# Attention two blocks at a time over two groups, with results in place

## The chip, the cores and the metric

One core of a Trainium2 chip runs the whole program. The metric is the device time of one execution in microseconds (us). The engines are PE (matrix products), DVE (vector), ACT (activations), POOL and SP, which issues the transfers. Each works through its own instructions in program order and waits on the others by semaphores.

## The reference

```python
# attention within chunks of 64: q, k, v are (8, 8, 576, 64)
scores = scale * np.matmul(q_c, k_c.transpose(0, 1, 2, 4, 3))
scores = scores - np.max(scores, axis=-1, keepdims=True)
attn = np.exp(scores)
attn = attn / (np.sum(attn, axis=-1, keepdims=True) + 1e-09)
out = np.matmul(attn, v_c)
# x: (4608, 512) from out
h = x @ w_in                     # 512 -> 2048
x2 = (h * np.cos(h)) @ w_out     # 2048 -> 512
a = x2 @ w1; b = x2 @ w2         # 512 -> 1024 each
y = ((a * b) @ w3) @ w_out2      # all float32
```

## The kernel before

The 4608 tokens are nine tiles of 512 (`TT`); a tile is four blocks of 128 tokens, and a block is two chunks of 64 for eight heads. Float32 products run as three products of split numbers (`mm3`, L104: high x high, high x low, low x high), so that an operand always has a high part (ACT copies it) and a low part (DVE or POOL subtracts).

The program has three parts. The first pass goes over all nine tiles with five of the eight weight groups each (`GA`, 45 groups in all); the second goes over the tiles with the other three; the last applies the second network. One group makes two halves of h (`d` and `e`), takes cos (`chain_t`, `chain_r`, `chain_cos`, `chain_g`: ACT, DVE, ACT, DVE), splits g = h cos h (`split_g`, copies on ACT, subtractions on POOL at L570), and one group later multiplies g with `w_out` in two output products `x` and `y` of 12 matmuls of 512 columns. h is formed with full products in the first two tiles (steps P, Q) and from tile 2 on with seven smaller ones (steps 1, 2, 5, 3 of 6, 12, 12, 12 matmuls of 256 columns).

The order of all instructions is written out: each group runs a string (`ORDER0` in tile 0, `ORDER1P` in tile 1, `ORDER1` in tiles 2 to 7; an E stands for the last group of a tile), one letter per step. Lower-case `a c b d` and capitals `A C B D` are the cos chain, `s` splits the previous group's g, `v` converts weights (tile 0), `l m h r` prepare later weights in four steps on ACT and DVE, `M H R` make sums of weights, `S T o` prepare the next tile's x.

Attention runs ahead of the products. Blocks 0 to 3 are done at the start (`START`). In each of the first four groups of a tile, one block of the next tile goes through five steps, at the five letters `q`:

- A, `att_scores` (L355): 32 matmuls 64x64x64 into two PSUM banks; for each of two banks a maximum over 64 (DVE, L367) and a subtraction (L369) into `ex`
- B, `att_softmax` (L373): the exponential, 512 elements per partition, in place (ACT, L375)
- E, `att_scale` (L377): sum, add, reciprocal (DVE), and the division, a multiplication on POOL (L384)
- C, `att_transpose` (L387): four transposes on PE (L391) and a copy on ACT into a second tile `pt` (L393)
- D, `att_values` (L396): 32 matmuls 64x64x64 (L404) and two copies of 256 elements into `xf` (ACT, L409)

In tiles 2 to 7, A stands between steps 2 and 5, B and E behind step 5, C between the two output products, D behind the second. The exponential and the sine use different tables on ACT, and a load of the table stands ahead of each change. q and k of a block are loaded on SP's queue at A of a block before, v at D of the block before.

PSUM has eight banks: four of `acc`, two of `h`, and two (`at`) that attention uses in turn for scores, transposes and values.

Of the kernel before, what the change touches and what calls it, by code (L numbers as in the profile page):

```python
# [9 lines left out]
F32 = mybir.dt.float32  # L10
# [4 lines left out]
ALU = mybir.AluOpType  # L15
# [41 lines left out]
def chunk_attention_two_ffn(  # L57
# [276 lines left out]
    qk_at = [0]  # L334

    def load_qk(j):
        qk_at[0] = j + 1
        qks[j] = t = wk.tile([P, 2, 2 * HP, 64], F32, tag="qk", name="qk")
        nc.sync.dma_start(out=t[:, 0], in_=q[j])
        nc.sync.dma_start(out=t[:, 1], in_=k[j])  # L340

    def load_v(j):
        vs[j] = vt = one.tile([P, 2, HP, 64], F32, tag="v", name="vt")
        for c in range(2):
            nc.sync.dma_start(out=vt[64 * c:64 * c + 64], in_=v[j].rearrange("(e t) c h d -> c t e h d", e=2)[c])

    def banks_of(j, early, name):
        return [(ps_acc.tile([P, HP, P], F32, tag=f"acc{2 * (j % 2) + c}", name=f"{name}{c}") if early and name == "ps_s"  # L350
                 else ps_h.tile([P, HP, P], F32, tag="h", name=f"{name}{c}") if early
                 else ps_at.tile([P, HP, P], F32, tag="at", name=f"{name}{c}"))[:, 0:2].rearrange("p a (b k) -> p (a b) k", k=64)
                for c in range(2)]

    def att_scores(j, early):  # L355
        qk = qks.pop(j)
        ps = banks_of(j, early, "ps_s")
        for h in range(2 * HP):
            for c in range(2):
                r, o = slice(64 * c, 64 * c + 64), 64 * (c ^ (h % 2))  # L360
                nc.tensor.matmul(ps[c][o:o + 64, h // 2], qk[r, 0, h], qk[r, 1, h], start=True, stop=True)
        while qk_at[0] < min(NJ, j + 2 + early):
            load_qk(qk_at[0])
        mx = small.tile([P, HP, 2], F32, tag="mx", name="mx")
        ex = wk.tile([P, HP, 2, 64], F32, tag="ex", name="ex")
        for c in range(2):
            nc.vector.reduce_max(out=mx[:, :, c], in_=ps[c], axis=AX.X)  # L367
        for c in range(2):
            nc.vector.tensor_tensor(out=ex[:, :, c], in0=ps[c], op=ALU.subtract,  # L369
                                    in1=mx[:, :, c].unsqueeze(2).to_broadcast([P, HP, 64]))  # L370
        att[j] = ex.rearrange("p h c k -> p (h c) k")

    def att_softmax(j, early):  # L373
        ex = att[j]
        nc.scalar.activation(ex, ex, AF.Exp, scale=SCALE)  # L375

    def att_scale(j, early):  # L377
        ex = att[j]
        sm = small.tile([P, 2 * HP], F32, tag="sm", name="sm")
        nc.vector.reduce_sum(out=sm, in_=ex, axis=AX.X)  # L380
        nc.vector.tensor_scalar_add(sm, sm, 1e-9)
        rc = small.tile([P, 2 * HP], F32, tag="rc", name="rc")
        nc.vector.reciprocal(rc, sm)
        (nc.vector if early else nc.gpsimd).tensor_tensor(  # L384
            out=ex, in0=ex, in1=rc.unsqueeze(2).to_broadcast([P, 2 * HP, 64]), op=ALU.mult)

    def att_transpose(j, early):  # L387
        ex = att[j]
        ps = bank(early)
        for h in range(HP):  # L390
            nc.tensor.transpose(ps[:, P * h:P * h + P], ex[:, 2 * h:2 * h + 2].rearrange("p e k -> p (e k)"), ident)  # L391
        pt = wk.tile([P, HP, P], F32, tag="ex", name="pt")
        nc.scalar.activation(pt, ps.rearrange("p (h t) -> p h t", h=HP), AF.Copy)  # L393
        att[j] = pt

    def att_values(j, early):  # L396
        pt = att.pop(j)
        ps = banks_of(j, early, "ps_v")
        vt = vs.pop(j)
        for h in range(HP):  # L400
            for e in range(2):
                for c in range(2):
                    r, o = slice(64 * c, 64 * c + 64), 64 * (c ^ e)
                    nc.tensor.matmul(ps[c][64 * e:64 * e + 64, h], vt[r, e, h], pt[r, h, o:o + 64], start=True, stop=True)  # L404
        n, jj = divmod(j, TT // P)
        if j + 1 < NJ:
            load_v(j + 1)
        for c in range(2):
            nc.scalar.activation(xf[:, :, P * jj + 64 * c:P * jj + 64 * c + 64], ps[c], AF.Copy)  # L409
        if jj == TT // P - 1 and n < NTILE - 1 and n not in xs:  # L410
            nc.sync.dma_start(out=xd[n], in_=xf)

    def att_tok(step, early):
        (att_scores, att_softmax, att_scale, att_transpose, att_values)["ABECD".index(step[0])](int(step[1:]), early)

    OPS = ("B11", "B21", "T2", "T1", "T3", "B22", "T4")
# [177 lines left out]
    def half_tile(c, name):  # L602
        return (one.tile([P, TT], F32, tag=("v", "x4")[c - 2], name=name) if c >= 2
                else wk.tile([P, TT], F32, tag="ex", name=name))

    xa = {}

    def load_x2a(n, c):
        xa[n, c] = t = half_tile(c, "x2a")
        nc.sync.dma_start(out=t, in_=x2a[n][c])  # L610


# [34 lines left out]

    def load_wf(f):
        if f in (2, 3):
            parts = tuple(wk.tile([P, TT], F32R, tag=("t", "ex")[f - 2], name="wf") for _ in range(2))  # L650
# [104 lines left out]
    with tc.manual_schedule():  # L755
# [10 lines left out]
        for tok in START.split():  # L766
            if tok == "x":
                conv_tick()
            elif tok == "o":
                x_op(plain.pop(0))  # L770
            else:
                att_tok(tok, True)

        def order_of(i, nth, end):
            if i < GA:
                return ORDER0E if end else ORDER0
            if i < 2 * GA:
                return ORDER1PE if end else ORDER1P
            if i <= iA:
                return ORDER1E if end else ORDER1  # L780
# [4 lines left out]
        steps = [s + str(j) for j in range(4, NJ) for s in "ABECD"]  # L785
        NG = len(groups)
        iA, iB = (NTILE - 1) * GA, NTILE * GA
        n_sums = 0
# [1 line left out]
        for i in range(NG):  # L790
# [35 lines left out]
            for op in order_of(i, nth, end):  # L826
# [26 lines left out]
                elif op in "1253PQ":  # L853
                    getattr(z, "step" + op)()
                elif op in "ac":
                    chain_t(i, z.d if op == "a" else z.e, "ac".index(op))
                elif op in "AC":
                    chain_r(i, z.d if op == "A" else z.e, "AC".index(op))
                elif op in "bd":
                    chain_cos(i, "bd".index(op))  # L860
                elif op in "BD":
                    chain_g(i, z.d if op == "B" else z.e, "BD".index(op))
                elif op == "q":
                    if i < iA and nth < 4:
                        att_tok(steps[20 * n + 5 * nth + n_q], False)
                    elif i >= iB + FOLD and fq < 4 * FB2:
                        need(("w3", fq // 2), *(("wo2", j) for j in range(FB2)))
                        fold(fq // 4, fq % 4)
                        fq += 1
                        if fq == 4 * FB2:  # L870
                            load_wf(0)
                            load_wf(1)
                    n_q += 1
                elif op in "ST":
                    x_sums("ST".index(op))
                elif op == "o":
                    if i < GA and not n_o:
                        x_plain()
                    x_op((z.done if i < GA or i >= 2 * GA else OPS)[n_o], n + 1 if ps == 0 else None)
                    n_o += 1  # L880
# [138 lines left out]
```

## Time and profile before

| | us |
|---|---|
| median of 3 runs | 1495.42 (1493.06 to 1502.28) |
| profiled execution | 1492.33 |
| its span in the trace | 1490.5 |

| engine | busy us | share of the span |
|---|---|---|
| PE | 1444.5 | 97% |
| DVE | 1094.4 | 73% |
| ACT | 687.4 | 46% |
| POOL | 264.7 | 18% |

The span is the time from the first to the last instruction of the profiled execution. Attention ends at about 545 us of it. PE's granted clock over the span is 0.989 of full; it is lower only in the first slices of the page (7, 8 and then 9 tenths or more). A busy PE counts from the start of a matmul to its modelled end; matmuls overlap, so the distance from one start to the next tells what one costs.

### The profile page before, as it was taken

The numbers are of one execution on the slowest core, as the hardware profiler recorded it, in microseconds if no ns is written. First come the engines' busy times: TensorE is split into PE (matmuls) and PEld (weight loads), VectorE is DVE, ScalarE is ACT, GpSimd is POOL, SyncE is SP. The second block draws the span as 40 slices with busy tenths as digits, with TensorE's granted clock in tenths as the row PEclk, the third lists the DMA queues.
The fourth block names the chain that finished last, engine by engine and source line by source line (L and its number), as shares of the span: only waits on it lengthen the run. The fifth ranks groups of instructions, "written<-read, shape, count | busy, mean of one in ns | idle before, by whom it ended". The sixth has DMA issues, their size and how long they took to land.

```text
span 1490.5 us, 26018 instructions
## 1 busy us (share of the span) xinstructions
PE 1444.5 (97%) x9996; PEld 1247.3 (84%) x9996; DVE 1094.4 (73%) x1844; ACT 687.4 (46%) x1173; POOL 264.7 (18%) x194
## 2 busy tenths in 40 slices
PE   5889999999999999999999999999999999999998
PEld 4778878888888889988888889998888888888887
DVE  6986789898898887777777777676565666656553
ACT  4776677777777775444444444231032023014002
POOL 0222222222222222211222222122000100200000
PEclk7899999999999999999999999999999999999999
DMA  7664656565664718999989684586435542641501
GB/s 247 205 206 142 214 175 216 168 242 186 220 229 145 248 65 290 372 336 322 312 290 343 243 305 144 196 328 247 148 113 192 169 148 109 224 148 59 212 34 57
DMA packets 122812, 307.38 MB, mean 206 GB/s; under 512 B 13632, under 2 KB 25664, under 8 KB 121536
## 3 DMA queue, kind: packets, MB, share of 16 engines
q1 hardware_dynamic: 122688, 305.71, 58.9%
q8 instruction: 79, 1.29, 0.3%
q14 instruction: 45, 0.37, 0.1%
HBM read 210.50 MB, written 95.16 MB: 205 GB/s over the span
## 4 chain that ended last, share of the span: by engine, by line
PE 77%; DVE 12%; ACT 4%; DMA 3%; issue 2%; POOL 1%; SPq 0%; DVEq 0%; ACTq 0%; POOLq 0%
PE acc L106 10%; PE acc L107 10%; PE acc L108 10%; PE ps_hh L106 10%; PE ps_hh L108 10%; PE ps_hh L107 9%; PE ps_aa L106 5%; PE ps_aa L107 5%; PE ps_aa L108 5%; ACT L375 2%; PE ps_v L404 1%; DVE ex L369 1%; DVE t L552 1%; POOL ex L384 1%; DVE sm L380 1%
## 5 line engine op out<-in xcount | busy, mean ns | idle before, releaser
L570 POOL TENSOR_TENSOR g<-t,g 128x512 fp32r<-128x512 f32 x144 | 198.9, 1402 | 557.8 <-ACT g L569 519.0
L106 PE MATMUL acc<-g,w 128*128 128x512 f32 x576 | 228.5, 397 | 0.0
L107 PE MATMUL acc<-g,w 128*128 128x512 f32 x576 | 225.9, 392 | 0.0
L108 PE MATMUL acc<-g,w 128*128 128x512 f32 x576 | 225.0, 391 | 0.0
L108 PE MATMUL ps_hh<-T,w 128*128 128x256 f32 (+1 forms) x616 | 181.8, 295 | 4.6 <-DVE w L199 4.6
L106 PE MATMUL ps_hh<-T,w 128*128 128x256 f32 (+1 forms) x616 | 184.7, 300 | 0.0
L107 PE MATMUL ps_hh<-T,w 128*128 128x256 f32 (+1 forms) x616 | 181.4, 295 | 0.0
L108 PEld LDWEIGHTS acc<-g,w 128*128 128x128 f32 x576 | 108.5, 188 | 23.6
L107 PEld LDWEIGHTS acc<-g,w 128*128 128x128 f32 x576 | 109.0, 189 | 19.9 <-POOL g L570 0.6
L106 PEld LDWEIGHTS acc<-g,w 128*128 128x128 f32 x576 | 108.9, 189 | 19.7
L108 PEld LDWEIGHTS ps_hh<-T,w 128*128 128x128 f32 x616 | 118.2, 192 | 7.7 <-DVE w L199 5.2
L106 PE MATMUL ps_hh<-B,w 128*128 128x256 f32 (+1 forms) x396 | 120.2, 304 | 3.7 <-DVE t L561 2.9
L106 PEld LDWEIGHTS ps_hh<-T,w 128*128 128x128 f32 x616 | 118.2, 192 | 5.4
L107 PEld LDWEIGHTS ps_hh<-T,w 128*128 128x128 f32 x616 | 118.3, 192 | 3.2
L107 PE MATMUL ps_hh<-B,w 128*128 128x256 f32 (+1 forms) x396 | 116.5, 294 | 0.0
L108 PE MATMUL ps_hh<-B,w 128*128 128x256 f32 (+1 forms) x396 | 116.3, 294 | 0.0
L744 ACT ACTIVATE phl<-e 128x512 fp32r<-128x512 f32 x32 | 20.2, 632 | 201.2 <-DVE e L742 201.2
L557 ACT ACTIVATE t<-t,half_pi 128x512 f32<-128x512 f32 x144 | 98.3, 715 | 1.4
L106 PE MATMUL acc<-wf,phl 128*128 128x512 f32 x252 | 98.2, 390 | 0.0
L107 PE MATMUL acc<-wf,phl 128*128 128x512 f32 x252 | 98.1, 389 | 0.0
L108 PE MATMUL acc<-wf,phl 128*128 128x512 f32 x252 | 98.0, 389 | 0.0
L547 ACT ACTIVATE t<-d 128x512 int32<-128x512 f32 x62 | 38.9, 627 | 120.6 <-DVE d L501 120.6
(199 smaller groups left out, 3417.4 us busy)
## 6 DMA issues: line engine op xcount, KB each, us to landing
w<-sd SPq DMA_DIRECT2D x159, 512.0 KB, 5.9
sd<-raw SPq DMA_DIRECT2D x104, 256.0 KB, 4.7
s<-sd SPq DMA_DIRECT2D x43, 256.0 KB, 5.2
qk<-in_q_dram SPq DMA_DIRECT2D x36, 256.0 KB, 4.4
qk<-in_k_dram SPq DMA_DIRECT2D x36, 256.0 KB, 4.6
vt<-in_v_dram SPq DMA_DIRECT2D x72, 128.0 KB, 3.2
x2a<-x2o SPq DMA_DIRECT2D x36, 256.0 KB, 3.2
x2a<-x2a SPq DMA_DIRECT2D x36, 256.0 KB, 5.6
```

The costliest lines, as they stand in the source:

```text
L106: nc.tensor.matmul(ps, a[0], b[0], start=first, stop=False)
L107: nc.tensor.matmul(ps, a[0], b[1], start=False, stop=False)
L108: nc.tensor.matmul(ps, a[1], b[0], start=False, stop=last)
L369: nc.vector.tensor_tensor(out=ex[:, :, c], in0=ps[c], op=ALU.subtract, in1=mx[:, :, c].unsqueeze(2).to_broadcast([P, HP, 64]))
L375: nc.scalar.activation(ex, ex, AF.Exp, scale=SCALE)
L380: nc.vector.reduce_sum(out=sm, in_=ex, axis=AX.X)
L384: (nc.vector if early else nc.gpsimd).tensor_tensor(out=ex, in0=ex, in1=rc.unsqueeze(2).to_broadcast([P, 2 * HP, 64]), op=ALU.mult)
L404: nc.tensor.matmul(ps[c][64 * e:64 * e + 64, h], vt[r, e, h], pt[r, h, o:o + 64], start=True, stop=True)
L547: nc.scalar.activation(t.bitcast(I32), h, AF.Copy, scale=INV2PI, bias=0.25)
L557: nc.scalar.activation(t, t, AF.Sin, scale=TWO_PI, bias=half_pi)
L570: nc.gpsimd.tensor_tensor(out=lo, in0=r, in1=f32(hi), op=ALU.subtract)
L744: nc.scalar.activation(t[:, 0], e0, AF.Copy)
```

## The change

Blocks 4 to 35 go in pairs: the first two groups of a tile take one pair, the next two another. The even group has one step (letter 6: scores of both blocks), in tiles 1 to 7 between its two output products and in tile 0 at its end. The odd group has the other four (7, 8, 9, 0): exponential right behind the split of g, division behind step 5 (or Q), transposes between the output products, values at the end. In the even group's string of tiles 1 to 7, the product of the first half with its cosine (`B`) now stands ahead of the weight step `m`, and `d` behind it.

One operation on DVE, ACT and POOL covers both blocks: two maxima and two subtractions of 512 elements per pair, one exponential, one sum and one division of 1024, two copies of 512 into `xf`. Transposes are copied per block, back into `ex`, which has one buffer of 4 KB in place of two of 2 KB. Both v of a pair are loaded right after the scores into a buffer of q and k; q and k of the next pair are loaded one after the scores and one after the values. The four early blocks keep their step order, and write to two unused weight slots. Tiles of later passes that shared the two `ex` buffers are halves of the one now; the small tiles have one buffer.

```diff
-ORDER0 = "PsvaAqQvqcCqxybBdvDqvq"
+ORDER0 = ("PsvaAQvcCxybBdvD6v", "Ps7vaAQ8vcCx9ybBdvD0v")
-ORDER1P = "PsqMhQqqHaclAxqbCrRmBdyqDL"
+ORDER1P = ("PsMhQHaclAxbCrRBm6dyDL", "Ps7MhQ8HaclAx9bCrRmBdy0DL")
-ORDER1 = "1s2qMh5qqHa3clAxqbCrRmBdyqDL"
+ORDER1 = ("1s2Mh5Ha3clAxbCrRBm6dyDL", "1s72h58Ha3clAx9bCrRmBdy0DL")
...
-    small = ctx.enter_context(tc.tile_pool(name="small", bufs=2))
+    small = ctx.enter_context(tc.tile_pool(name="small", bufs=1))
...
+    def load_v2(j):
+        vt = wk.tile([P, 2, 2, HP, 64], F32, tag="qk", name="vt2")
+        for b in range(2):
+            vs[j + b] = vt[:, b]
+            fill_v(vt[:, b], j + b)
...
+    def less_max(ex, ps):
+        g = ex.shape[1]
+        mx = small.tile([P, 2, g], F32, tag="mx", name="mx")
         for c in range(2):
+            nc.vector.reduce_max(out=mx[:, c], in_=ps[c], axis=AX.X)
...
+    def over_sum(ex, eng):
+        e = ex.rearrange("p g c k -> p (g c) k")
...
+        eng.tensor_tensor(out=e, in0=e, in1=rc.unsqueeze(2).to_broadcast([P, g, 64]), op=ALU.mult)
...
+    def turn(ex, ps):
         for h in range(HP):
+            nc.tensor.transpose(ps[:, P * h:P * h + P], ex[:, h].rearrange("p e k -> p (e k)"), ident)
+        nc.scalar.activation(ex.rearrange("p h c k -> p (h c k)"), ps, AF.Copy)
...
+    def pair_tok(step, j):
+        if step == "A":
+            att[j] = ex = wk.tile([P, 2 * HP, 2, 64], F32, tag="ex", name="ex", bufs=1)
+            ps = pair_banks("ps_s")
+            for b in range(2):
+                scores_mm(qks.pop(j + b), ps, b)
+            load_v2(j)
+            if j + 2 < NJ:
+                load_qk(j + 2)
+            less_max(ex, ps)
+        elif step == "B":
+            nc.scalar.activation(att[j], att[j], AF.Exp, scale=SCALE)
+        elif step == "E":
+            over_sum(att[j], nc.gpsimd)
+        elif step == "C":
+            for b in range(2):
+                turn(att[j][:, HP * b:HP * b + HP], bank(False))
+        else:
+            ex = att.pop(j)
+            ps = pair_banks("ps_v")
+            for b in range(2):
+                values_mm(ex[:, HP * b:HP * b + HP], vs.pop(j + b), ps, b)
+            if j + 3 < NJ:
+                load_qk(j + 3)
...
+            for c in range(2):
+                nc.scalar.activation(x[:, c], ps[c].rearrange("p (b h) k -> p b h k", b=2), AF.Copy)
...
+        if c == 0:
+            t = wk.tile([P, 2, TT], F32, tag="ex", name="x2a", bufs=1)
...
+                elif op in "67890":
+                    if i < iA and nth < 4:
+                        pair_tok("ABECD"["67890".index(op)], 4 * n + 4 + nth // 2 * 2)
```

## Rows read from the trace of the kernel before

**Rows 1.** Part 1 of the page: busy us (share of span) and instructions of each engine.

```profile
PE 1444.5 (97%) x9996; PEld 1247.3 (84%) x9996; DVE 1094.4 (73%) x1844; ACT 687.4 (46%) x1173; POOL 264.7 (18%) x194
```

**Rows 2.** Stretches: length, busy PE, PEld, DVE, ACT, POOL; clock, DMA share, GB/s.

```profile
34.20:111.08 76.88, 65.35 (x620) 58.22 (x619) 72.13 (x119) 54.64 (x91) 18.23 (x14) 0.93 0.66 214
111.08:168.20 57.12, 54.16 (x562) 46.63 (x561) 39.82 (x84) 39.05 (x66) 14.57 (x13) 1.00 0.47 150
420.10:481.87 61.77, 61.54 (x605) 53.31 (x604) 52.82 (x97) 46.34 (x77) 18.10 (x15) 1.00 0.57 197
```

**Rows 3.** Part 4 of the page: shares of the chain that ended last, by line.

```profile
PE acc L106 10%; PE acc L107 10%; PE acc L108 10%; PE ps_hh L106 10%; PE ps_hh L108 10%; PE ps_hh L107 9%; PE ps_aa L106 5%; PE ps_aa L107 5%; PE ps_aa L108 5%; ACT L375 2%; PE ps_v L404 1%; DVE ex L369 1%; DVE t L552 1%; POOL ex L384 1%; DVE sm L380 1%
```

**Rows 4.** PE's timeline around one block: start us, us, engine, line, operation, out<-in, count.

```profile
455.93 0.28 PE L108 MATMUL ps_hh<-T,w 128*128 128x256 f32 x1
456.14 0.69 PE L361 MATMUL ps_s<-qk 64*64 64x64 f32 x32
456.76 0.39 PE L106 MATMUL ps_hh<-T,w 128*128 128x256 f32 x1
456.98 0.28 PE L107 MATMUL ps_hh<-T,w 128*128 128x256 f32 x1
457.10 0.28 PE L108 MATMUL ps_hh<-T,w 128*128 128x256 f32 x1
...
462.26 0.39 PE L108 MATMUL acc<-g,w 128*128 128x512 f32 x1
462.73 0.66 PE L391 MATMUL ps_at<-ident,ex 128*128 128x128 f32 x4
463.14 0.47 PE L106 MATMUL acc<-g,w 128*128 128x512 f32 x1
463.45 0.39 PE L107 MATMUL acc<-g,w 128*128 128x512 f32 x1
...
465.76 0.39 PE L108 MATMUL acc<-g,w 128*128 128x512 f32 x1
466.08 0.69 PE L404 MATMUL ps_v<-pt,vt 64*64 64x64 f32 x32
466.70 0.39 PE L106 MATMUL ps_hh<-B,w 128*128 128x256 f32 x1
466.93 0.28 PE L107 MATMUL ps_hh<-B,w 128*128 128x256 f32 x1
```

**Rows 5.** The other engines' timeline in the same block.

```profile
455.85 2.53 POOL L570 TENSOR_TENSOR g<-t,g 128x512 fp32r<-128x512 f32 x2 [6.06 <-ACT g L569]
...
456.90 0.75 DVE L367 TENSOR_REDUCE mx<-ps_s 128x4 f32<-128x256 f32 x2
...
458.39 1.28 ACT L375 ACT_TABLE_LOAD   x1 [1.64 <-DVE ex L369]
...
458.50 0.69 DVE L499 TENSOR_TENSOR e<-d,ps_hh 128x512 f32<-128x512 f32 x1 [0.18 <-PE ps_hh L108]
...
459.22 0.42 DVE L501 TENSOR_TENSOR d<-e,ps_hh 128x256 f32<-128x256 f32 x1
...
460.35 0.69 DVE L380 TENSOR_REDUCE sm<-ex 128x8 f32<-128x512 f32 x1 [0.71 <-ACT ex L375]
...
461.63 1.04 POOL L384 TENSOR_TENSOR ex<-ex,rc 128x512 f32<-128x512 f32 x1 [3.25 <-DVE rc L383]
...
461.95 1.27 DVE L552 SCALAR_TENSOR_TENSOR t<-d,t 128x512 f32<-128x512 f32 x1
...
464.79 0.69 DVE L264 SCALAR_TENSOR_TENSOR cw<-raw,cw 128x512 uint32<-128x512 uint32 x1
```

**Rows 6.** The list of waits: us in total, times, longest us.

```profile
PEld ps_at L391 <- POOL ex L384: 19.3, 29, 4.4
...
PE ps_hh L106 <- DVE t L561: 2.9, 4, 0.9
```

**Rows 7.** Part 6 of the page, DMA issues: count, KB each, median us to landing.

```profile
qk<-in_q_dram SPq DMA_DIRECT2D x36, 256.0 KB, 4.4
```

More of the change, by code (lines that the diff above doesn't have):

```diff
@@ L340, in load_qk, with fill_v, scores_mm @@
         nc.sync.dma_start(out=t[:, 1], in_=k[j])
+    def fill_v(vt, j):
+        for c in range(2):
+            nc.sync.dma_start(out=vt[64 * c:64 * c + 64], in_=v[j].rearrange("(e t) c h d -> c t e h d", e=2)[c])
     def load_v(j):
         vs[j] = vt = one.tile([P, 2, HP, 64], F32, tag="v", name="vt")
[L344 to L357, printed above, removed]
+        fill_v(vt, j)
+    def load_v2(j):
[3 more added lines that the diff above has]
+            fill_v(vt[:, b], j + b)
+    def scores_mm(qk, ps, b):
         for h in range(2 * HP):
@@ L360, in att_scores @@
                 r, o = slice(64 * c, 64 * c + 64), 64 * (c ^ (h % 2))
[L361 to L365, printed above, removed]
+                nc.tensor.matmul(ps[c][o:o + 64, HP * b + h // 2], qk[r, 0, h], qk[r, 1, h], start=True, stop=True)
@@ L373, in att_softmax @@
[L373 to L380, printed above, removed]
+                                    in1=mx[:, c].unsqueeze(2).to_broadcast([P, g, 64]))
+    def over_sum(ex, eng):
+        e = ex.rearrange("p g c k -> p (g c) k")
+        g = e.shape[1]
+        sm = small.tile([P, g], F32, tag="sm", name="sm")
+        nc.vector.reduce_sum(out=sm, in_=e, axis=AX.X)
@@ L381, in att_scale @@
         nc.vector.tensor_scalar_add(sm, sm, 1e-9)
-        rc = small.tile([P, 2 * HP], F32, tag="rc", name="rc")
+        rc = small.tile([P, g], F32, tag="rc", name="rc")
         nc.vector.reciprocal(rc, sm)
[L384 to L389, printed above, removed]
-        for h in range(HP):
[L391 to L394, printed above, removed]
@@ L403, in att_values @@
                     r, o = slice(64 * c, 64 * c + 64), 64 * (c ^ e)
[L404 to L410, printed above, removed]
-            nc.sync.dma_start(out=xd[n], in_=xf)
@@ L413, in att_tok, with keep_x, early_tok @@
-    def att_tok(step, early):
-        (att_scores, att_softmax, att_scale, att_transpose, att_values)["ABECD".index(step[0])](int(step[1:]), early)
+                    nc.tensor.matmul(ps[c][64 * e:64 * e + 64, HP * b + h], vt[r, e, h], pt[r, o:o + 64],
+                                     start=True, stop=True)
+    def keep_x(n):
+        if n < NTILE - 1 and n not in xs:
+            nc.sync.dma_start(out=xd[n], in_=xf)
+    first_ex = {}
+    def early_tok(step, j):
+        if step == "A":
+            if j % 2 == 0:
+                first_ex[j // 2] = wpool.tile([P, 2 * HP, 2, 64], F32, tag=f"w{NSLOT - 1 - j // 2}", name="ex0")
+            att[j] = first_ex[j // 2][:, HP * (j % 2):HP * (j % 2) + HP]
+            ps = [ps_acc.tile([P, 2 * HP, 64], F32, tag=f"acc{2 * (j % 2) + c}", name=f"ps_s{c}")[:, 0:HP]
+                  for c in range(2)]
+            scores_mm(qks.pop(j), ps, 0)
+            load_qk(j + 2)
+            less_max(att[j], ps)
+        elif step == "B":
+            nc.scalar.activation(att[j], att[j], AF.Exp, scale=SCALE)
+        elif step == "E":
+            over_sum(att[j], nc.vector)
+        elif step == "C":
+            turn(att[j], bank(True))
+        else:
+            ps = [ps_h.tile([P, 2 * HP, 64], F32, tag="h", name=f"ps_v{c}")[:, 0:HP] for c in range(2)]
+            values_mm(att.pop(j), vs.pop(j), ps, 0)
+            if j < 3:
+                load_v(j + 1)
+            for c in range(2):
+                nc.scalar.activation(xf[:, :, P * j + 64 * c:P * j + 64 * c + 64], ps[c], AF.Copy)
+            if j == 3:
+                keep_x(0)
@@ new lines, in pair_banks @@
+    def pair_banks(name):
+        return [ps_at.tile([P, 2 * HP, 64], F32, tag="at", name=f"{name}{c}") for c in range(2)]
+    def pair_tok(step, j):
+        if step == "A":
+            att[j] = ex = wk.tile([P, 2 * HP, 2, 64], F32, tag="ex", name="ex", bufs=1)
[4 more added lines that the diff above has]
+            if j + 2 < NJ:
+                load_qk(j + 2)
+            less_max(ex, ps)
+        elif step == "B":
+            nc.scalar.activation(att[j], att[j], AF.Exp, scale=SCALE)
+        elif step == "E":
+            over_sum(att[j], nc.gpsimd)
+        elif step == "C":
+            for b in range(2):
+                turn(att[j][:, HP * b:HP * b + HP], bank(False))
+        else:
+            ex = att.pop(j)
[4 more added lines that the diff above has]
+                load_qk(j + 3)
+            n, jj = divmod(j, TT // P)
+            x = xf[:, :, P * jj:P * jj + 2 * P].rearrange("p h (b c k) -> p c b h k", b=2, c=2)
+            for c in range(2):
+                nc.scalar.activation(x[:, c], ps[c].rearrange("p (b h) k -> p b h k", b=2), AF.Copy)
+            if jj == 2:
+                keep_x(n)
@@ L600, in x2_mm @@
                 nc.sync.dma_start(out=x2d[n][:, c], in_=t)
-    def half_tile(c, name):
-        return (one.tile([P, TT], F32, tag=("v", "x4")[c - 2], name=name) if c >= 2
-                else wk.tile([P, TT], F32, tag="ex", name=name))
     xa = {}
     def load_x2a(n, c):
-        xa[n, c] = t = half_tile(c, "x2a")
+        if c == 0:
+            t = wk.tile([P, 2, TT], F32, tag="ex", name="x2a", bufs=1)
+            xa[n, 0], xa[n, 1] = t[:, 0], t[:, 1]
+        elif c > 1:
+            xa[n, c] = one.tile([P, TT], F32, tag=("v", "x4")[c - 2], name="x2a")
+        t = xa[n, c]
         nc.sync.dma_start(out=t, in_=x2a[n][c])
@@ L649, in load_wf @@
         if f in (2, 3):
-            parts = tuple(wk.tile([P, TT], F32R, tag=("t", "ex")[f - 2], name="wf") for _ in range(2))
+            d = wk.tile([P, 2, TT], F32R, tag="ex", name="wf", bufs=1) if f == 3 else None
+            parts = (d[:, 0], d[:, 1]) if f == 3 else tuple(wk.tile([P, TT], F32R, tag="t", name="wf") for _ in range(2))
             for i in range(2):
@@ L783, in order_of @@
             return (ORDER3X if nxt in xs else ORDER3E) if end else ORDER3B if nth else ORDER3
-        steps = [s + str(j) for j in range(4, NJ) for s in "ABECD"]
         NG = len(groups)
```

23 lines of the change are left out of this document (7 added, 16 removed).

## The prediction

> **What bounds the kernel now.** I read the page's busy times first: PE is busy 97% of the span, DVE 73% [rows 1]. An average over stages with different limits says little, so I cut the stretch with attention, the first 545 us, by token tiles [rows 2]. In tile 0 (34.20 to 111.08) DVE is busy 72.13 of 76.88 us and PE 65.35: DVE sets the pace. Tile 1 (111.08 to 168.20) is bound by neither (PE 54.16, DVE 39.82 of 57.12): waits along a chain. In a settled tile (420.10 to 481.87) PE is busy 61.54 of 61.77 us, DVE 52.82, ACT 46.34: PE is the bound, and a change there pays only in PE's own slots. The chain of waits names the softmax (ACT L375 2%, DVE L369, L380 and POOL L384 1% each [rows 3]); that looks like 75 us to be had, but the chain merely follows whoever released PE last.
>
> What PE really loses to one block stands in its timeline [rows 4]. A 256-column product takes 0.12 us (456.98 to 457.10), a 512-column one 0.23 (462.26 is the last of x, and 463.45 to 465.76 holds ten). Against these, scores cost 0.09 before (455.93 + 0.12 to 456.14) and 0.10 after (456.76 to 456.98 instead of 0.12); transposes 0.24 before (462.49 to 462.73) and 0.08 after (463.14 to 463.45); values 0.09 before (465.99 to 466.08) and 0.11 after. Together 0.71 us per block, 1.42 per two. Of it only the 0.24 is a wait, for POOL's division: 462.67, when it ends [rows 5], to 462.73. The list of waits agrees: 29 such, 19.3 us on the weight-load side [rows 6].
>
> **The change, part by part.** Products and transposes stay the same in number.
>
> *Entries and exits of PE.* Each kind is entered once per two blocks. What is left is 0.09 + 0.10 for scores, 0.08 behind the transposes, 0.09 + 0.11 for values: 0.47 us, and W, the wait ahead of the transposes. The gain is 1.42 - 0.47 - W = 0.95 - W per pair. There are twelve pairs in tiles 2 to 7 and two each in tiles 0 and 1.
>
> *W.* In the odd group no scores stand between steps 2 and 5, and steps 5, 3 and x are as before. So the transposes are due 3.99 us after DVE's addition e of step 5 begins (458.50 to 462.49). In that time come e and d (to 459.22 + 0.42, 1.14 us), then the sum, the small operations and the hand-over to POOL (0.59 us, 461.04 to 461.63), the division, and 0.06 to PE. The sum over 1024 elements is not in the trace: 0.69 at 512 is its floor, 1.38 its ceiling; two of 256 take 0.75 against 0.69 for one of 512, so I take 1.25. The division over 1024 lies between 1.04 (length free) and 2.08 (all length); two operations of 512 on POOL take 2.53 where one needs half of that, so I take 2.08. Sum: 1.14 + 1.25 + 0.59 + 2.08 + 0.06 = 5.12, and W = 1.13. With the floor for the division W is 0.09, with both ceilings 1.26. The exponential, 0.65 at 512 (table ready 459.67, sum begins 460.35), is no later: its load of 1.28 and some 1.1 of work now follow the copies of g directly, end about with d, and have more cover than before. In the first pair of a tile they come later: the even group's second output product closes the previous tile, and two copies on ACT and two on DVE (0.69 each, as e) go ahead of the last product of g. I add 0.7 there: W = 1.8.
>
> *Tiles 2 to 7.* The second pair costs 1.13 - 0.95 = +0.2, the first 1.8 - 0.95 = +0.85: +1.05 per tile, +6.3 us.
>
> *Shorter queues.* Per pair DVE saves some 0.4 on maxima and subtractions (0.75 for two maxima [rows 5], subtractions alike, so 3.0 now; four of 512 at 0.6 to 0.69 then) and 0.7 on the sum (2 x 1.28 against 1.84). Against it stands POOL: DVE's operation on t at 461.95 took 1.27 and ended 0.55 after POOL's [rows 5]; a division of 2.08 can hold it 1.76 us where two held it 1.44. Only tile 0 is paid in DVE time: 2 x (1.1 - 0.3) = -1.6 us. ACT saves one of two exponential table loads and one of two sine loads per pair, 2.6 us; in settled tiles that is idle time, so it counts nothing.
>
> *Tile 1.* Here the first product of a group waits for its bank, released by DVE L561 (4 such waits in the kernel, 2.9 us, up to 0.9 [rows 6]). In the even group this product of g now stands ahead of the three weight operations instead of behind them, so that wait of 0.9 goes; in the odd one it stays. Per pair -0.9 - 0.95 + 1.13 = -0.7, for two -1.4.
>
> *The start.* One load of v is gone and the four early blocks no longer share two buffers; at least 0, at most about 1: -0.5.
>
> *What counts nothing, and its cover.* The burst of four DVE operations ends the even group's queue with g's last product behind it. From the start of x on, PE still has 2.75 + 0.19 + 1.24 + 2.75 = 6.9 us; DVE then has e, two remainders, one low part, a product (0.69 each), three weight operations (at most 0.69 each, 2.1 [rows 5]), the burst (2.6) and g: 8.8. So g ends about 1.9 into the next group. Its x comes 42 x 0.12 = 5.0 in and needs a copy (0.6), POOL (1.27) and hand-overs (0.15) before: g has until 3.0. The margin of 1.1 covers it. Two copies of transposes (1.2 us) hide under y (2.75). Loads: as many as before on SP, in other places; v goes with the scores, a group ahead of its use, and the pair's second q and k follow the values, 8 us ahead of the scores, where a load lands in 4.4 [rows 7]. In-place results need no transfer; the memory of the later passes is cut up otherwise, but used a group or more apart.
>
> *Sum.* 6.3 - 1.6 - 1.4 - 0.5 = +2.8 us on the profiled execution's 1492.33: 1495.1. The median of the runs shown, 1495.42, is 3.1 higher, so against it I write 1498.2.
>
> A rule that points the other way: the Trainium skill, "ScalarE: Activation LUTs", section "What ACT_TABLE_LOAD costs", puts a switch of tables at 2.66 us with its drain, and says to batch calls by set. Here the load takes 1.28 and the exponential follows it within 0.02 of its end [rows 5]. By the page 32 loads less would free 85 us of ACT, by the row 41.
>
> **The rivals.**
>
> *A, faster: the division isn't late.* If the 1024-element division costs little over 1.04, W is about 0.1. Then each pair gains 0.85: 12 x 0.85 + 3.5 = 13.7, 1481.7 against the median. For it: nothing in the trace shows this form at 1024. Against it: POOL's other operations show no fixed part.
>
> *B, slower: g's last product is late in every pair.* Its place is the end of the even group. If it ends over 3.0 us into the odd group, that group's x waits, and POOL, which makes the low part of g, takes the division later too. It decides from 1.1 us of extra DVE delay; a three-part weight (four more operations, some 1.7) or the two copies of the first pair eat that. Were it 1.2 us late in all twelve pairs: +14, 1512. For it: DVE is 86% busy in settled tiles and POOL holds it. The Trainium skill, "SBUF — State Buffer", section "Who interferes with whom", says that the later of the two engines is blocked for the whole instruction; the operation at 461.95 agrees for an operation with both inputs in SBUF. Against it: only three weights in this stretch have three parts.
>
> *C, much faster: the table loads were on the path.* The chain gives ACT L375 2% of the span, 30 us: 1468. Against it: PE is idle 0.23 of 61.77 us there, and the wait ahead of the transposes is 0.24 a block, which the softmax alone could give back. By the rule of the Trainium skill told above, to batch by set, this is what the change would give.
>
> **How the numbers follow.** My forecast has 0.66, with a range of its own of 1491 to 1505 (W between 1.0 and 1.3, 0.3 to 1.2 more in first pairs, tile 0 and the start off by 3 us). A has 0.17 (1477 to 1489), B 0.14 (1505 to 1516), C 0.03. The range of 1482 to 1508 holds nearly all of the forecast, over half of A and a quarter of B: 0.79 to 0.8. Within 1% (1480.5 to 1510.4, about what a measurement of this kernel can tell from no change) lies 0.85; faster 0.08 (the low end of A, and C), slower 0.07 (the high half of B).
>
> **What would show it.** Transposes wait for POOL's division 1.1 us per odd group, 1.8 in the first pair of a tile: some 25 us in the list of waits; even groups take about 11.9 us, odd ones 13.8 to 14.5. The division takes 2.1 us, the sum 1.25. Table loads fall by about half. Tile 0 is 1 to 2 us shorter. If the wait is under 0.3, A holds; if x in odd groups waits for POOL's low part, B. I am wrong if pass 2 or the last part changes length, for nothing there was counted.

## The result and the profile after

The changed kernel takes 1509.0 us (median of 6 runs, 1507.35 to 1510.78), the kernel before beside it 1495.33 (6 runs, 1492.11 to 1502.28): a ratio of 1.0081, 95% interval 1.0064 to 1.0097. It is 0.8% slower. The forecast was 1498.2. By the medians the measured time lies 1.0 above the upper end of the range, and inside the 1% for which the prediction had 0.85; the ratio, put on the 1495.42 that the forecast started from, gives 1507.5, just inside the range.

The profiled execution took 1510.13, its span 1508.3. Part 1 of its page answers to [rows 1]:

```profile
PE 1438.8 (95%) x9996; PEld 1249.1 (83%) x9996; DVE 1091.3 (72%) x1732; ACT 641.9 (43%) x1095; POOL 266.2 (18%) x178
```

PE, DVE and ACT are less busy than before, by 5.7, 3.1 and 45.5 us, while the span is 17.8 longer. So the time went into waiting. To find where, I cut the first pass at the first product of each tile. The first two stretches of [rows 2] began some 2.3 us behind those cuts, and the second ended 9 us before tile 1 did. Here are tiles 0 and 1 of the kernel before with the right cuts (columns as in [rows 2]):

```profile
31.93:108.80 76.87, 65.34 (x609) 58.21 (x610) 73.49 (x121) 54.80 (x92) 16.91 (x12) 0.91 0.66 216
108.80:177.25 68.45, 65.49 (x634) 57.00 (x633) 46.25 (x94) 46.94 (x79) 17.60 (x14) 1.00 0.45 146
```

And tiles 0, 1, 2 and 6 of the kernel after:

```profile
32.69:118.08 85.39, 66.52 (x608) 59.53 (x609) 69.46 (x107) 51.78 (x84) 15.26 (x10) 0.92 0.58 192
118.08:182.05 63.97, 63.53 (x633) 56.56 (x632) 48.36 (x80) 40.90 (x69) 17.17 (x12) 1.00 0.50 165
182.05:250.57 68.52, 60.67 (x603) 53.12 (x602) 59.17 (x96) 42.27 (x72) 16.90 (x12) 1.00 0.51 171
440.90:503.65 62.75, 60.37 (x603) 53.02 (x602) 52.46 (x84) 40.35 (x68) 18.35 (x12) 1.00 0.57 193
```

PE's granted clock in tile 0 is 0.92, where it was 0.91, so the clock is not what makes the tile longer. In the table the last column runs from the first product of tile 8 to the start of the last product of all.

| us | start | tile 0 | 1 | 2 | 3 | 4 | 5 | 6 | 7 | rest |
|---|---|---|---|---|---|---|---|---|---|---|
| before | 31.93 | 76.87 | 68.45 | 65.20 | 61.87 | 62.23 | 61.87 | 61.77 | 61.76 | 933.5 |
| after | 32.69 | 85.40 | 63.97 | 68.52 | 63.45 | 63.45 | 63.45 | 62.74 | 62.75 | 936.8 |
| change | +0.8 | +8.5 | -4.5 | +3.3 | +1.6 | +1.2 | +1.6 | +1.0 | +1.0 | +3.3 |
| predicted | -0.5 | -1.6 | -1.4 | +1.05 | +1.05 | +1.05 | +1.05 | +1.05 | +1.05 | 0 |

Up to the last part the sum is +14.5, which the medians (+13.7) confirm. The last column I take for scatter: the twelve profiles of the experiments, in which that part is as in the change, have 931.7 to 935.1 there. In tile 0 DVE has 4.0 us less to do than before and idles 15.9 us instead of 3.4.

PE's list of waits after (engine, operation and line, releaser; us in total, times, longest) answers to [rows 6]:

```profile
PE ps_at L382 <- POOL ex L377: 17.3, 14, 1.8
PE ps_hh L108 <- DVE w L199: 15.8, 7, 3.2
PE ps_hh L106 <- DVE d L526: 6.6, 4, 2.5
```

The first row is PE's idle part of the prediction's W (W itself is counted from one start of a product to the next and is 0.16 more in each wait); some 25 us had been expected. The second row is waits of tile 0's products for a converted weight's low part. The list of tile 0 of the kernel before has:

```profile
PE ps_hh L108 <- DVE w L199: 4.6, 2, 3.1
PE ps_at L391 <- POOL ex L384: 4.2, 1, 4.2
PE ps_v L404 <- ACT pt L393: 2.7, 4, 0.7
```

The growth of the first of them by 11.2 is the surprise; the other two are gone from tile 0, and a single wait of 2.8 for a weight's high part has come. The third row after belongs mostly to tile 2.

W itself, in tile 6, in one timeline of all engines (start, us, engine, line, operation; in brackets the idle time before and its releaser); it answers to [rows 4, 5]:

```profile
456.57 1.28 ACT L440 ACT_TABLE_LOAD   x1
457.12 0.69 DVE L536 TENSOR_TENSOR e<-d,ps_hh 128x512 f32<-128x512 f32 x1 [0.64 <-PE ps_hh L108]
457.87 1.06 ACT L440 ACTIVATE ex<-ex 128x1024 f32<-128x1024 f32 x1
458.96 1.22 DVE L373 TENSOR_REDUCE sm<-ex 128x16 f32<-128x1024 f32 x1 [0.69 <-ACT ex L440]
460.82 1.90 POOL L377 TENSOR_TENSOR ex<-ex,rc 128x1024 f32<-128x1024 f32 x1 [2.52 <-DVE rc L376]
461.14 2.13 DVE L589 SCALAR_TENSOR_TENSOR t<-d,t 128x512 f32<-128x512 f32 x1
462.78 1.09 PE L382 MATMUL ps_at<-ident,ex 128*128 128x128 f32 x8 [1.50 <-POOL ex L377]
```

The sum waits 0.69 for the exponential and takes 1.22 (1.25 expected), the division takes 1.90 (2.08 expected), and the transposes start 0.06 behind its end, as they did before the change. PE waits 1.5.

### The profile page after: what moved, and what is told of

Read it like the earlier page. It is cut to its first block, busy times and chain, and to the rows that moved or that the text cites. A ratio compares the mean times of both kernels' runs of the same rounds, so it can differ in the third digit from the quotient of the medians.

```text
span 1508.3 us, 25782 instructions
## 1 busy us (share of the span) xinstructions
PE 1438.8 (95%) x9996; PEld 1249.1 (83%) x9996; DVE 1091.3 (72%) x1732; ACT 641.9 (43%) x1095; POOL 266.2 (18%) x178
## 4 chain that ended last, share of the span: by engine, by line
PE 74%; DVE 14%; ACT 5%; DMA 4%; issue 2%; POOL 2%; SPq 0%; DVEq 0%; ACTq 0%; POOLq 0%
PE ps_hh L106 10%; PE ps_hh L108 10%; PE ps_hh L107 9%; PE acc L106 9%; PE acc L107 9%; PE acc L108 9%; PE ps_aa L106 5%; PE ps_aa L107 5%; PE ps_aa L108 5%; POOL ex L377 2%; DVE t L598 1%; PE ps_v L391 1%; DVE sm L373 1%; DVE mx L364 1%; PE ps_at L382 1%
## 5 line engine op out<-in xcount | busy, mean ns | idle before, releaser
L607 POOL TENSOR_TENSOR g<-t,g 128x512 fp32r<-128x512 f32 x144 | 202.9, 1429 | 675.6 <-ACT g L606 638.4
L108 PEld LDWEIGHTS ps_hh<-T,w 128*128 128x128 f32 x616 | 119.8, 194 | 15.2 <-DVE w L199 12.7
L106 PEld LDWEIGHTS ps_hh<-T,w 128*128 128x128 f32 x616 | 119.9, 195 | 3.2
L107 PEld LDWEIGHTS ps_hh<-T,w 128*128 128x128 f32 x616 | 119.9, 195 | 3.2
L594 ACT ACTIVATE t<-t,half_pi 128x512 f32<-128x512 f32 x144 | 98.2, 714 | 1.4
L606 ACT ACTIVATE g<-t 128x512 fp32r<-128x512 f32 x144 | 86.2, 630 | 24.6 <-DVE t L598 17.9
```

The costliest lines, as they stand in the source:

```text
L106: nc.tensor.matmul(ps, a[0], b[0], start=first, stop=False)
L107: nc.tensor.matmul(ps, a[0], b[1], start=False, stop=False)
L108: nc.tensor.matmul(ps, a[1], b[0], start=False, stop=last)
L594: nc.scalar.activation(t, t, AF.Sin, scale=TWO_PI, bias=half_pi)
L606: nc.scalar.activation(hi, r, AF.Copy)
L607: nc.gpsimd.tensor_tensor(out=lo, in0=r, in1=f32(hi), op=ALU.subtract)
```

## The experiments

All start from the changed kernel. Tile lengths are measured as in the table above, each from one profiled run; line numbers in rows are those of the run's own kernel. Ratios are to the kernel before, run beside each experiment; its medians went from 1495.3 to 1498.6 between the rounds, so a difference of two medians taken apart is good to some 3 us.

**e1, one block at a time, in place, one buffer.** The old orders are back in every tile, and so are the loads of v block by block; results still go in place and `ex` still has one buffer of 4 KB, its halves used in turn.

```diff
+ORDER0S = "PsvaAqQvqcCqxybBdvDqvq"
+ORDER1PS = "PsqMhQqqHaclAxqbCrRmBdyqDL"
+ORDER1S = "1s2qMh5qqHa3clAxqbCrRmBdyqDL"
+SINGLE = (0, 1, 2, 3, 4, 5, 6, 7)
...
+            att[j] = first_ex["one"][:, HP * (j % 2):HP * (j % 2) + HP]
...
```

> One block per group in every tile, with the steps at the places of the kernel before; only the memory of the change is kept (results in place in one 4 KB ex buffer, one buffer of the small tiles, early blocks in weight slots). Theory (the loss of 14 us comes from the pairing: tile 0 longer by 8.5 us, waits ahead of the transposes in tiles 2 to 7): in place costs nothing, 1495 us, within 3 us of the kernel before. Rival (fewer buffers and copies into the tile that PE reads make new waits): 1503 us or more.

Measured: 1488.43 (1485.74 to 1495.74), ratio to the kernel before 0.9946 (0.9927 to 0.9965). Working in place costs nothing; what I had not expected is that it gains some 8 us over the kernel before by the ratio, 0.5 to 1.0 in each of tiles 3 to 7 (61.22 to 61.25). So all of the change's loss, and some 8 us more, is in the pairs and their places. (The profiled run was the slowest of the eight, at 1495.74: its first product came 3.1 later than before and its tile 0 took 81.92, so that only the other tiles are read from it. Tiles 1 to 7 are 5.2 shorter together.)

**e2, blocks one at a time in tile 0 alone.**

```diff
+SINGLE = (0,)
...
-                return ORDER0E if end else ORDER0[nth % 2]
+                return ORDER0E if end else ORDER0S if i // GA in SINGLE else ORDER0[nth % 2]
```

> Tile 0 one block per group at the places of before, pairs in tiles 1 to 7. Theory (tile 0 itself loses 8.5 us): tile 0 lasts 77 us instead of 85, the rest is unchanged, 1500 to 1501 us. Rival (the time is only moved: the weights that come late in tile 0 are waited for later anyway): tile 0 shorter, but tiles 1 and 2 longer by as much, 1507 to 1510 us.

Measured: 1500.37 (1498.01 to 1505.16), ratio 1.0024 (1.0010 to 1.0037). That is 8.6 us under the changed kernel; tile 0 took 76.92 and the tiles behind it what they took in the changed kernel to 0.02 us. So the loss of tile 0 is its own, as the theory had it.

**e3, the pair's division on DVE instead of POOL.**

```diff
-            over_sum(att[j], nc.gpsimd)
+            over_sum(att[j], nc.vector)
```

> The change with its division of 1024 on DVE instead of POOL. Theory (in tiles 2 to 7 PE waits for the division at the transposes, 1.0 to 1.7 us per odd group beyond the entry of 0.1): the division takes about 1.25 instead of 2.1 and needs no hand-over, so the wait falls by 0.9 to 1.0 in 12 to 14 pairs, -10 to -14 us: 1495 to 1499 us, tile 0 still 84 to 86 us. Rival for tile 0 (POOL's long division blocks DVE's operations there): tile 0 also falls to 80 us or less. Rival for tiles 2 to 7 (DVE is late anyway, not POOL): no more than 3 us gained, 1506 to 1509.

Measured: 1500.17 (1497.41 to 1503.37), ratio 1.0020 (1.0005 to 1.0035), 8.8 less than the changed kernel, short of the 10 to 14 expected. Tiles 2 to 7 lost 1.0 to 1.4 each (62.0 in tiles 3 to 5, 61.3 in tiles 6 and 7). PE's waits:

```profile
PE ps_hh L108 <- DVE w L199: 16.1, 7, 3.2
PE ps_hh L106 <- DVE d L526: 7.1, 3, 3.0
PE ps_at L382 <- DVE ex L377: 7.0, 9, 1.1
```

PE's waits for the division fall from 17.3 to 7.0: the larger part of W was the length of POOL's division, which took 1.93 on POOL and 1.23 on DVE (means of 16). But tile 0 took 88.0, with the same 16 us of waits for weights. That speaks against the hold of DVE by POOL's division, which is to be seen there (below), as the cause of tile 0's loss; it is no proof, since the division now takes DVE's own time. e10 settles it.

**e4, tile 0's pairs at other places.** Scores of the pair behind A, and the other four steps later in the odd group.

```diff
-ORDER0 = ("PsvaAQvcCxybBdvD6v", "Ps7vaAQ8vcCx9ybBdvD0v")
+ORDER0 = ("PsvaA6QvcCxybBdvDv", "PsvaAQv7cC8xybBdvD9v0")
```

> The change, but in tile 0 the steps of the pair stand where the five letters stood in the kernel before: scores between P and Q of the even group, in the odd one the exponential behind Q, the sum and division behind c C, transposes and values at the end. Theory (tile 0 loses because its DVE queue has no work of attention at the points where it waits for ACT's half of the cosine): with the places given back tile 0 takes 79 to 82 us, 1503 to 1506 us. Rival (pairing itself costs it: the operations of 1024 are too long and one group of two has none): tile 0 stays at 84 to 86 us, 1508 to 1510.

Measured: 1500.03 (1498.28 to 1501.91), ratio 1.0019 (1.0006 to 1.0032); tile 0 took 78.33. That is more than the 3 to 6 us expected back. Not the pairing but the places cost tile 0 its time. Four more runs take the places apart.

**e8, only the even group's place of e4.**

```diff
-ORDER0 = ("PsvaAQvcCxybBdvD6v", "Ps7vaAQ8vcCx9ybBdvD0v")
+ORDER0 = ("PsvaA6QvcCxybBdvDv", "Ps7vaAQ8vcCx9ybBdvD0v")
```

> The changed kernel, but in tile 0 the even group's pair of scores stands right behind A, as in the kernel of which tile 0 took 78.3 us; the odd group's order is as in the changed kernel. It tells which half of the moved places costs the 8.5 us of tile 0. Theory: the burst at the end of the even group holds back the weight's low parts (the next product waits for them), so most of it returns here: tile 0 near 81, time 1503. Rival: the odd group's order (division ahead of the converted weights, chain behind it) is what costs; then tile 0 stays at 84 or more and the time within 2 us of 1509.

Measured: 1507.64 (1505.47 to 1510.1), ratio 1.0075 (1.0058 to 1.0092), tile 0 84.43. My theory of the burst at the end of the even group fell; the rival holds.

**e9, only the odd group's places of e4.**

```diff
-ORDER0 = ("PsvaAQvcCxybBdvD6v", "Ps7vaAQ8vcCx9ybBdvD0v")
+ORDER0 = ("PsvaAQvcCxybBdvD6v", "PsvaAQv7cC8xybBdvD9v0")
```

> The changed kernel, but in tile 0 the odd group's four steps (exponential, sum with division, transposes, values) stand where the kernel with tile 0 at 78.3 us has them; the even group's scores stay at the end, as in the change. With the kernel whose even group alone was moved (tile 0 at 84.4) it completes the square. Theory after that run: the odd group's order carries the 8 us, since a weight's low part there queues behind the sum and behind the DVE operation that POOL's division holds; tile 0 near 79 to 80 and the time 1501 to 1503. Rival: the two halves only pay together, each removing a wait that the other would put in its place; then tile 0 stays at 83 or more and the time at 1506 or more.

Measured: 1498.97 (1498.04 to 1502.09), ratio 1.0014 (1.0000 to 1.0028), tile 0 78.45. The odd group's places carry all of it. The reason given there, the sum and POOL's hold on DVE, is tested next.

**e10, only the transposes and values later.** Exponential and sum stay early, as in the change. The transposes go behind D and the values to the very end, which are the places that steps C and D had in the kernel before.

```diff
-ORDER0 = (..., "Ps7vaAQ8vcCx9ybBdvD0v")
+ORDER0 = (..., "Ps7vaAQ8vcCxybBdvD9v0")
```

> The changed kernel, but in tile 0's odd group only the transposes and the values are later, the transposes behind the last product of g and the values at the very end, so that their copies on ACT stand behind the converted weights' ones; the exponential and the sum with its division stay early. If the copies on ACT are what holds the weights back, tile 0 falls to about 80 us and the time to 1503. If it is the sum and the division on the DVE queue, tile 0 stays at 84 or more and the time within 2 us of 1509.

Measured: 1499.25 (1494.98 to 1500.69), ratio 1.0019 (1.0004 to 1.0033), tile 0 75.95, 0.9 shorter than before. So the sum and the division, which stayed early, cost nothing there: one or both of the two later steps did, and with more returned than the 80 us expected of the copies on ACT.

**e12, only the values later.**

```diff
-ORDER0 = (..., "Ps7vaAQ8vcCx9ybBdvD0v")
+ORDER0 = (..., "Ps7vaAQ8vcCx9ybBdvDv0")
```

> The changed kernel, but in tile 0's odd group only the values and their two copies of x are one place later, behind the last converted weight; the transposes stay between x and y as in the change. The kernel with both later ran at 1499.3 with tile 0 at 76.0. Theory: ACT's copies of the transposes stand ahead of the sine's and wait for PE's transposes, which wait for POOL's division; DVE then waits for the sine, and the weight's last part behind it is late. It is the transposes' place, so nothing returns here: tile 0 stays at 83 to 86 and the time within 2 us of 1509. Rival: the values' copies ahead of the last converted weight hold it; then tile 0 falls to 76 to 78 and the time to 1500.

Measured: 1508.92 (1508.25 to 1510.12), ratio 1.0069 (1.0052 to 1.0086), tile 0 87.80. Nothing returns, so the place of the transposes is needed for all of the gain. (Transposes later without the values was not run, and neither were the copies later without the transposes: that it is the copies on ACT is read from the traces.)

The trace of the changed kernel shows how, in the first odd group of tile 0 (timeline of DVE, ACT, POOL and PE, the other products left out):

```profile
55.54 2.16 POOL L377 TENSOR_TENSOR ex<-ex,rc 128x1024 f32<-128x1024 f32 x1 [7.04 <-DVE rc L376]
55.85 2.12 DVE L125 TENSOR_SCALAR cw<-raw 128x512 uint32<-128x512 uint32 x1
57.81 1.04 PE L382 MATMUL ps_at<-ident,ex 128*128 128x128 f32 x8
...
58.51 1.09 ACT L383 ACTIVATE ex<-ps_at 128x512 f32<-128x512 f32 x2 [2.59 <-PE ps_at L382]
...
59.22 0.68 DVE L589 SCALAR_TENSOR_TENSOR t<-ps_hh,t 128x512 f32<-128x512 f32 x1
59.62 1.28 ACT L594 ACT_TABLE_LOAD   x1
60.91 1.33 ACT L594 ACTIVATE t<-t,half_pi 128x512 f32<-128x512 f32 x2
...
61.67 0.69 DVE L598 TENSOR_TENSOR t<-t,ps_hh 128x512 f32<-128x512 f32 x1 [1.76 <-ACT t L594]
...
62.88 0.42 DVE L125 TENSOR_SCALAR cw<-raw 128x512 uint32<-128x512 uint32 x1
```

ACT reaches the copy of the transposes (L383) and stands 2.59 us until PE has made them. The table load and the sine of the cos chain (L594) come behind it in ACT's order, though they need nothing of attention. DVE is through with L589 at 59.90 and waits 1.76 for the sine, and behind that product of g (L598) stands the rest of the weight's conversion, for which products of tile 0 wait. The same stretch in e10 (timelines of ACT and of DVE):

```profile
57.03 2.13 DVE L125 TENSOR_SCALAR cw<-raw 128x512 uint32<-128x512 uint32 x1
58.35 1.28 ACT L594 ACT_TABLE_LOAD   x1
59.65 0.73 ACT L594 ACTIVATE t<-t,half_pi 128x512 f32<-128x512 f32 x1
60.40 0.68 DVE L589 SCALAR_TENSOR_TENSOR t<-ps_hh,t 128x512 f32<-128x512 f32 x1
61.00 0.68 DVE L598 TENSOR_TENSOR t<-t,ps_hh 128x512 f32<-128x512 f32 x1
```

POOL's division holds L125 there just as long, but the sine is ready and L598 follows L589 without a wait. The list of waits in tile 0 after:

```profile
PE ps_hh L108 <- DVE w L199: 15.8, 7, 3.2
DVE t L589 <- ACT t L584: 7.1, 6, 2.2
DVE t L598 <- ACT t L594: 5.3, 3, 2.2
ACT ex L383 <- PE ps_at L382: 5.2, 2, 2.6
```

And the list of waits in tile 0 of e10:

```profile
PE ps_hh L108 <- DVE w L199: 6.9, 3, 3.0
DVE t L589 <- ACT t L584: 3.7, 4, 1.2
DVE t L598 <- ACT t L594: 1.3, 1, 1.3
ACT ex L383 <- PE ps_at L382: 0.7, 1, 0.7
```

With the transposes later, ACT's wait for PE goes from 5.2 to 0.7, DVE's for ACT from 12.4 to 5.0, and PE's for weights from 15.8 to 6.9 (8.9 less, beside 9.4 by which the tile is shorter). In e12 ACT's wait is again 5.2 and PE's 15.5.

**e5, the burst on the scores behind the last product of g** (even groups, all tiles; `4` is the new letter).

```diff
-ORDER1 = ("1s2Mh5Ha3clAxbCrRBm6dyDL", ...)
+ORDER1 = ("1s2Mh5Ha3clAxbCrRBm6dyD4L", ...)
-            less_max(ex, ps)
+            late["ps"] = ps
+        elif step == "M":
+            less_max(att[j], late["ps"])
```

> The pairs stay as in the changed kernel, but the even group's four DVE operations on the scores (two maxima, two subtractions, 2.7 us) are issued behind the last product of g instead of ahead of it. Theory: in tile 2 the burst together with the three-part weights' operations makes d late (waits of PE for d of 2.7 and 1.9 us in the odd groups); without it these waits go, tile 2 falls from 68.5 to about 65 us, the other tiles stay within 0.6 of 63.4 because the division over 1024 elements still ends late: 1504, 4 to 6 us under the changed kernel's 1509. Rival 1: d is late because of the weights' operations alone; then tile 2 stays at 68.5 and the time at 1509. Rival 2: the exponential starts later by as much as the burst was moved, so W rises from 1.6 to over 2.5 us in each pair: some 1520.

Measured: 1505.93 (1503.27 to 1507.28), ratio 1.0057 (1.0040 to 1.0073). The 3 us are there, but not where I expected: tile 2 fell by 1.2 only, tiles 3 to 5 by 0.7, tiles 6 and 7 not at all. In tile 2 two waits for d are left:

```profile
PE ps_hh L106 <- DVE d L530: 4.7, 2, 3.1
PE ps_at L382 <- POOL ex L377: 0.5, 1, 0.5
```

The waits for d total 4.7, where the changed kernel had 4.1 for d and 3.6 for the division. What the edit moves is g's last product, ahead of the burst; the burst itself stands ahead of the next group's d on the DVE queue in both kernels. So the edit could not take the wait for d away, and in tiles 3 to 7 it brings one of 0.8 in the first pair; what shrinks is the wait for the division. That the burst makes d late is therefore neither shown nor refuted.

**e6, three pieces together:** tile 0 one block at a time (e2), division on DVE (e3), burst late (e5).

> Three pieces together: blocks one at a time in tile 0 (in place in one buffer, as in the kernel with the old places there), pairs in tiles 1 to 7, their division on DVE, and the burst issued behind the last product of g. Theory: the costs are separate (tile 0 8.6 us, the division on POOL 8.8, the burst 4 to 5), so they add: 1509 - 8.6 - 8.8 - 4 = 1488, tile 0 near 77, tile 2 near 64, tiles 6 and 7 near 61.3. Rival: the division on DVE had already brought tile 2's d forward or the burst's move costs W what it saves; then 1492 or more.

Measured: 1491.67 (1487.57 to 1493.67), ratio 0.9956 (0.9941 to 0.9970). That is between the sum and the rival. Tiles 6 and 7 are the 61.3 expected, tile 1 63.87; tile 2 took 66.85, not 64. The three single runs gave 8.6, 8.8 and 3.1, which would make 1488.5, so 3.2 us are missing and the costs add up only roughly. Tile 0 took 80.92 in the profile, which is of the slowest of the nine runs (1493.67).

**e7, the table loaded early,** on the kernel of e1.

```diff
             less_max(att[j], ps)
+            nc.scalar.activation(small.tile([P, 1], F32, tag="dm", name="dm"), ident[:, 0:1], AF.Exp)
```

> Blocks one at a time with one buffer in place (the kernel that ran at 1488.4), and a one-column Exp of a constant issued on ACT ahead of the softmax's Exp, at the end of step A, so that the table is loaded before DVE's subtraction is done. Theory: what is left of W there (0.28 us in every other group) is the table load of 1.28 us standing behind the subtraction; then the load moves ahead, the waits of the transposes go in all groups, each tile is 0.5 us shorter, and the time 1485, 3 to 4 us under. Rival: the division on POOL is late for another reason (DVE's queue); then the time stays at 1488, or is a little longer for the extra instruction.

Measured: 1487.87 (1484.25 to 1490.53), ratio 0.9937 (0.9920 to 0.9955). The groups of instructions have the loads ahead of the exponential (count; busy, mean ns; idle before); in the kernel before:

```profile
L375 ACT ACT_TABLE_LOAD x31 | 39.8, 1283 | 31.7 <-DVE ex L369 31.5
```

In e1:

```profile
L444 ACT ACT_TABLE_LOAD x31 | 39.8, 1283 | 9.7 <-DVE ex L370 9.3
```

In e7:

```profile
L443 ACT ACT_TABLE_LOAD x31 | 39.8, 1283 | 0.5
```

The load no longer waits for the subtraction, and tiles 3 to 7 take 60.93 to 60.99, 0.25 less than in e1 where I had said 0.5. Over six tiles that would be 1.5 us, and the medians (0.6 apart) can't resolve it. Between the kernel before and e1 most of the load's wait went with the other buffer, which is where I see e1's gain; why the load waits with one placing of the buffer and not with the other isn't shown.

**e11, e7 with the pairs kept in tile 1 alone,** where they gain.

```diff
-SINGLE = (0, 1, 2, 3, 4, 5, 6, 7)
+SINGLE = (0, 2, 3, 4, 5, 6, 7)
```

> The kernel that ran at 1487.9 (one block at a time, one buffer in place, the table loaded early) with the pairs of the change kept in tile 1 alone, where the changed kernel took 64.0 us and that one 66.7. Theory: a tile's gain or loss stays its own; tile 1 about 64, tile 2 about 64.2 as there, so 2.7 us under it: 1485. Rival: the pairs of tile 1 only push the wait into tile 2, as the sum of the two tiles in the kernel with everything in pairs but tile 0 (63.9 + 66.9, against 66.7 + 64.2) may be read; then the time stays at 1488.

Measured: 1489.15 (1483.13 to 1492.85), ratio 0.9944 (0.9922 to 0.9966). In the profile tiles 1 and 2 take 63.97 + 64.81 against e7's 66.74 + 64.17, 2.1 less; the medians don't show it. Inconclusive. The best version is e7 or e1, both ahead of the kernel before and of the change.

## Why the prediction came out as it did

**What bounds the kernel: right for settled tiles, wrong for tile 0.** There I read "DVE is busy 72.13 of 76.88 us and PE 65.35: DVE sets the pace" [rows 2] and concluded that tile 0 is paid in DVE time. DVE's time did fall, by 4.0 us where I had counted 1.6, and the tile grew by 8.5.

**The step that failed: "Only tile 0 is paid in DVE time: 2 x (1.1 - 0.3) = -1.6 us."** I costed the operations that tile 0 sheds and never walked its new order. There the transposes move from behind D to between the output products, and their copies come ahead of the sine on ACT. The prediction put these copies at nothing because they "hide under y": PE indeed did not wait for them, but the sine did, and behind it DVE and the weights. Tile 0 is 10.1 of the 11.7 us between my sum and the tiles; e10 gives 9.4 of it back. The other misses (start +1.3, tile 1 -3.1, tiles 2 to 7 +3.4) nearly cancel, which is luck. With the transposes and values back at their old places (e10) tile 0 is 0.9 shorter than before in the one profile, near the -1.6.

**Entries and exits, W: right in mechanism, near in size.** In tile 6 of the changed kernel the even groups take 12.40 and 11.91 us, the odd ones 14.31 and 13.53 (before: 12.51, 12.89, 12.90, 12.88). The first pair so costs +1.3 and the second -0.3, where I had +0.85 and +0.2: together +1.0. That this meets the +1.05 is luck, as the two misses cancel. W is 1.7 in first pairs (1.8 predicted); in second pairs 0.9 in tiles 6 and 7 and 1.6 in tiles 3 to 5 (1.13 predicted), which is their +1.2 to +1.6. The cause of the 0.7 between them is the condition that rival B named, paid through the division: in tiles 3 to 5 the even group ahead makes three low parts of a weight (L294) and not one, g's last product comes later, and its copy on ACT, which stands ahead of the exponential, waits 0.69 for it. Adding the division's 2.08 at full length was right: 16 of them average 1.93. In e3 the wait shrinks with it.

**Tile 1: right direction, a third of the measured -4.5.** I removed one wait of 0.9 per pair and charged W of 1.13. With full products (P, Q of 24 matmuls each) the division has more time: W is 0.3 to 0.4 there, and the wait for the bank left all groups (the list of waits has it once, 0.2 us).

**Tile 2: rival B, in two of its places.** In its two odd groups PE waited 2.5 and 1.6 us for d, since the sums of weights and the weight step went ahead of the burst and g's last product: the case that B named (weights with more parts eat the margin), but in one tile and not in twelve pairs. What was late first was d, the addition of step 2, which has to free its bank for step 3, and not x. The first of the two, in the timelines of DVE and PE:

```profile
195.60 1.28 DVE L364 TENSOR_REDUCE mx<-ps_s 128x8 f32<-128x512 f32 x2
196.80 1.28 DVE L366 TENSOR_TENSOR ex<-ps_s,mx 128x512 f32<-128x512 f32 x2
197.99 1.28 DVE L629 COPY x2o<-acc 128x512 f32<-128x512 f32 x2
199.19 0.68 DVE L598 TENSOR_TENSOR t<-t,e 128x512 f32<-128x512 f32 x1
199.79 0.68 DVE L526 TENSOR_TENSOR d<-x,ps_hh 128x512 f32<-128x512 f32 x1
200.52 0.39 PE L106 MATMUL ps_hh<-B,s 128*128 128x256 f32 x1 [2.47 <-DVE d L526]
```

DVE has no idle time before d here, and the prediction had reckoned the margin for g alone.

**Rivals A and C fell.** W is not 0.1. Of the loads ahead of exponentials and sines, 63 became 33 and ACT lost 45 us of work, yet none of tiles 2 to 7 got shorter. The Trainium skill, "ScalarE: Activation LUTs", section "Table sets: the hidden batching unit", advises to batch calls by set; done here for pairs, it gave nothing that those tiles show. Each load still took 1.28. To let a load begin earlier (e7) took 0.25 off each of tiles 3 to 7 in the profile.

**The cover** held for transfers, which were not waited for in tiles 1 to 7, and the later passes kept their length but for the scatter named above. The margin of 1.1 for g's last product did not hold in tile 2.

## What to carry to other kernels

An engine that is 94% busy is not by that the bound: with written-out orders, walk the moved instruction through every queue that it enters, and ask what stands behind it that could already have run. A copy that waits for another engine belongs behind the work on its queue that waits for nothing of it. Price every place of a moved step by itself, even where the step seems to need only spare time.

## What the runs showed of the hardware that I had not expected

- A table load of 1.28 us that waits for the data of the operation behind it can be brought forward with a one-column operation of the same table: ACT's idle time before the loads fell from 9.7 us to 0.5 (e1, e7).
- While POOL divided (2.16 us from 55.54), DVE's one-input operation L125 took 2.12 us; it takes 0.42 where POOL does not work (62.88 in the same view). In e10 it is held as long (2.13), and tile 0 is short all the same. The Trainium skill, "SBUF — State Buffer", section "Who interferes with whom", lists this kind of operation among those that can contend with GpSimd (POOL) for the shared ports; the row agrees.
- Tile 0 with one block at a time took 76.9 to 77.9 us in four profiles (before, e2, e7, e11) and 80.9 and 81.9 in two (e6, e1), in these with two waits of 3.1 for a converted weight. With the odd group's steps at the change's places it took 84.4 to 88.0 in five profiles. What selects between them stays open; a single profile of tile 0 is not good to 5 us, and the verdicts on it above rest on the medians.
